# Three blocks of a fused retention and channel-mix kernel in 64-token chunks, and a new written order

## The chip, the cores and the metric

The kernel runs on one core of a Trainium2 chip. The metric is the time of one execution in microseconds on that core; runs of the kernel before gave 152.86 to 153.04 with a median of 152.95. PE is the matrix engine, DVE the vector engine, ACT the scalar engine; POOL (GpSimd) and SP issue the transfers here.

## The reference

Two layers follow each other. The first is a retention layer with 4 sequences, 8 heads, 768 tokens and a head size of 64: each head holds a 64x64 state that decays by a factor per token.

```python
state = gamma[None, :, None, None] * state + np.einsum('bhd,bhe->bhde', k[:, :, t], v[:, :, t])
y[:, :, t] = scale * np.einsum('bhd,bhde->bhe', q[:, :, t], state)
```

Its output, laid out as x of 4 x 768 x 512, goes through a channel mix:

```python
xk = mu_k * x + (1.0 - mu_k) * x_prev      # x_prev: x one token earlier
xr = mu_r * x + (1.0 - mu_r) * x_prev
k = np.maximum(xk @ w_k, 0.0)              # 512 -> 1024
v = k * k @ w_v                            # 1024 -> 512
r = 1.0 / (1.0 + np.exp(-(xr @ w_r)))
return r * v
```

Inputs and output are float32, and the products run on 16-bit operands.

## The kernel before

The 3072 tokens are worked in twelve blocks of 256; blocks 0 to 2 are the first sequence, 3 to 5 the second, and so on. `first(n)` is true for blocks 0, 3, 6 and 9, whose incoming state is zero; `more(n)` is false for 2, 5, 8 and 11, behind which no state is needed.

**The pieces.** A block goes through pieces with short names, each one function of the kernel. Loads `lq`, `lk`, `lv` bring q, k and v in. `vs` multiplies v by the decay of its place in the block. `Tq` and `Tk` turn q and k on PE into PSUM, and `Eq` and `Ek` copy the turned tiles back to 16 bits. `S` forms scores, `M` masks them into `a`. `C` forms the k-v products of each chunk, `U` adds them up to the state that is carried (`TG`, or `T32` for the last), and `G` decays it for the next block. `I`, `Y` and `J` form the output in PSUM: `I` and `J` from the carried state, `Y` from masked scores and values; where `Y` ends with the second half of the carried products, no `J` is written. `D` scales the output into `xT`. `dx` takes the difference of neighbouring tokens, `X.n.0.j` and `X.n.1.j` form the four pieces of xk and of xr. `K` multiplies by w_k, `Qa` and `Qb` apply relu and square on ACT, `R` and `s` form the gate, `V` multiplies by w_v, `O` multiplies by the gate, `st` stores. Blocks 3 and 4, 6 and 7, 9 and 10 share their mix products (`GROUPS`): `K.3`, `K.6` and `K.9` work on 512 tokens at once.

**Three ways to work a block.** Which one a block takes is set by tuples at the top. A block in neither `HALF` nor `WIDE` (0 and 1) has its tokens interleaved in pairs. A block in `WIDE` is cut into two chunks of 128 tokens, a block in `HALF` into four of 64.

- Scores: `WIDE` makes two pieces `S.n.0`, `S.n.1` of 8 products each, 64 rows by 128 columns on 128 tokens (L331), with one mask of 128x1024 for each (L354). `HALF` makes one piece of 32 products of 64x64 (L318), with one mask of 128x1024 (L347).
- State products: 8 or 16 with 128 rows (L384) against 24 or 32 with 64 rows (L366). `WIDE` adds up in two steps, `U.n.0` and `U.n.1`, `HALF` in four (three where no state follows), L419.
- Output: `WIDE` has `I`, `Y` with 16 products (L478) and `J`; `HALF` has `I` and a `Y` with 32 products (L462) that ends with what `J` does. The carried products stand on L441 in both. `D` is one operation of 128x1024 in `WIDE` (L514) and two of 128x512 in `HALF` (L507).
- Turning: a block in `WHOLE` has 16 products of 128 rows for each of q and k (L272), any other 32 of 64x64 (L278).

**The order.** No scheduler places the pieces. The kernel walks a string, `ORDER`, word by word, and each word issues one piece onto one engine's queue:

```python
for word in ORDER.split():
    word, _, at = word.partition("@")
    word, _, eng = word.partition("~")
    ...
    CODES[code](ENG.get(eng), *args)
```

`K.2.2@5` is a product into PSUM bank 5, `U.3.0~a` a sum on ACT; `~v` is DVE, `~p` POOL, `~s` SP. Each engine takes its own words in the order of the string and waits where an operand, a PSUM bank or a buffer isn't free. So the string decides what stands behind a waiting instruction. Buffers go round: four each of q, k and v, three of `vs`, of turned q and k and of `a`, four gates and four results.

Of the kernel before, what the change touches and what calls it, by code (L numbers as in the profile page):

```python
# [42 lines left out]
J.4 D.4~v dx.4~v R.2.0@6 Qb.2.1~a V.0.0.1 O.0.0~v X.3.0.1~v Eq.5~a Qb.1.2~a V.1.0.1 X.3.0.2~v
O.1.0~v Tq.6@01 Eq.6~a Tk.6@45 Ek.6~a st.0.0~s lk.7~p st.1.0~s V.1.1.0@3 V.1.1.1 O.1.1~v s.2.0~a
R.2.1@0 s.2.1~a lv.5~p X.3.0.0~v X.3.0.3~v Tk.7@67 Ek.7~a G.4~a S.6@45 M.6~v Tk.5@23 Ek.5~a vs.5~v
V.2.0.0@0 K.3.2@1 Qa.3.2~a K.3.0@6 S.5.0@23 M.5.0~v S.5.1@45 C.5@1 U.5.0~v K.3.3@7 Qb.3.2~a Qa.3.0~a
lq.7~p K.3.7@6 Qa.3.3~a Qa.3.7~a lv.6~p lq.8~p vs.6~v M.5.1~v V.2.0.1 st.0.1~s I.5@67 O.2.0~v
st.2.0~s C.6@23 U.6.0~a U.6.1~v U.6.2~v K.3.6@1 Qa.3.6~a lk.9~p X.3.1.3~v Y.5 Tq.7@45 Eq.7~a U.6.3~v
X.3.1.2~v I.6@01 J.5 X.3.1.0~v D.5~v X.3.1.1~v Qb.3.3~a G.6~a V.2.1.0@2 K.3.1@3 V.2.1.1 O.2.1~v
Qb.3.7~a Qa.3.1~a Qb.3.1~a dx.5~v K.3.4@4 K.3.5@5 Qa.3.5~a X.5.0.0~v X.5.0.3~v R.3.1@2 s.3.1~a  # L50
lv.7~p Qa.3.4~a X.5.0.1~v Qb.3.4~a R.3.0@5 R.4.0@2 s.3.0~a s.4.0~a Qb.3.0~a X.5.0.2~v vs.7~v K.5.2@4
S.7@67 st.1.1~s M.7~v Qb.3.5~a Y.6 Qb.3.6~a lv.10~p C.7@23 U.7.0~v X.5.1.1~v Qa.5.2~a K.5.0@5
R.4.1@6 Qa.5.0~a D.6~v s.4.1~a V.4.0.0@4 V.4.0.1 V.3.1.0@5 U.7.1~v Qb.5.0~a X.5.1.3~v U.7.2~v I.7@01
X.5.1.2~v U.7.3~v Tq.8@67 Eq.8~a X.5.1.0~v O.4.0~v lv.8~p vs.8~v Qb.5.2~a lq.10~p lk.8~p Tk.8@23
Ek.8~a V.3.1.1 V.3.0.0@4 C.8@67 O.3.1~v st.2.1~s st.3.1~s Y.7 dx.6~v D.7~v Tq.10@23 V.3.0.1 Eq.10~a
G.7~a dx.7~v X.6.0.2~v V.4.1.0@5 R.5.1@2 s.5.1~a K.5.3@0 Qa.5.3~a R.5.0@2 U.8.0~v O.3.0~v V.4.1.1
lv.9~p lk.10~p lq.9~p Tk.10@01 s.5.0~a U.8.1~v X.6.0.1~v Ek.10~a X.6.0.0~v Tk.9@23 Ek.9~a K.5.1@7
Qa.5.1~a X.6.0.3~v K.6.0@4 lq.11~p Qb.5.1~a Qa.6.0~a U.8.2~v I.8@01 vs.9~v S.8@23 M.8~v O.4.1~v
st.4.1~s K.6.4@7 Qa.6.4~a vs.10~v X.6.1.2~v K.6.2@6 C.9@23 Qa.6.2~a Qb.6.2~a U.9.0~a Y.8 U.9.1~v
D.8~v U.9.2~v U.9.3~v X.6.1.3~v Qb.5.3~a Tq.9@45 V.5.1.0@6 V.5.1.1 O.5.1~v Eq.9~a lk.11~p K.6.3@7  # L60
# [739 lines left out]
```

## Time and profile before

| | us |
|---|---|
| median of three runs | 152.95 |
| lowest, highest | 152.86, 153.04 |
| the profiled execution, its own time | 153.06 |
| span of that profile (first to last instruction) | 151.3 |
| PE busy | 143.5 |
| DVE busy | 127.5 |
| ACT busy | 103.4 |
| POOL busy | 55.3 |

The page gives times in microseconds, and mean durations of a group in nanoseconds. A line such as "L331 PE MATMUL ps<-qT,kT" names the kernel's line, the engine, the operation and what it writes from what. In a timeline the first number is the start, the second the time from the first start to the last end of so many like instructions, and a bracket holds idle time ahead of them and what ended it. The ends of products are modelled: a product's busy time is longer than the distance to the next one.

### The profile page before, as it was taken

How to read it: one execution, taken by the hardware profiler on the slowest of the kernel's cores; microseconds unless marked ns; L12 is line 12 of the kernel's file. 1: busy time of each engine (PE TensorE's matmuls, PEld its weight loads, DVE VectorE, ACT ScalarE, POOL GpSimd, SP SyncE). 2: the span in 40 equal slices, each digit the busy share in tenths (PEclk: the TensorE clock that was granted, in tenths of full speed). 3: DMA queues.
4: the chain of work that ended last, by engine and by line, in shares of the span. 5: the costliest groups of instructions: out<-in, count | busy, mean ns of one | idle time of the engine just before them, and what ended most of it. 6: DMA issues, size and time to landing. Idle time of an engine off the chain costs nothing.

```text
span 151.3 us, 5540 instructions
## 1 busy us (share of the span) xinstructions
PE 143.5 (95%) x2426; PEld 82.9 (55%) x2426; DVE 127.5 (84%) x212; ACT 103.4 (68%) x195; POOL 55.3 (37%) x65
## 2 busy tenths in 40 slices
PE   7878799999999999999999999999999999999991
PEld 3355487657754554547465564548456444655450
DVE  6976999999989999999999999999799999400432
ACT  3565979899844895879567786999504756839420
POOL 7954999479857209997700000000000000000000
PEclk9999999999999999999999999999999999999999
DMA  5999999999999999999999019311000005500433
GB/s 126 235 230 194 208 228 195 167 247 215 196 166 203 233 260 119 269 289 197 230 172 122 6 45 281 100 41 39 0 4 0 4 0 215 201 0 0 153 129 139
DMA packets 45624, 22.16 MB, mean 146 GB/s; under 512 B 37400, under 2 KB 41248, under 8 KB 45600
## 3 DMA queue, kind: packets, MB, share of 16 engines
q0 software_dynamic: 38704, 14.42, 74.5%
q1 hardware_dynamic: 6592, 7.21, 14.4%
q8 instruction: 19, 0.31, 0.8%
q10 hardware_dynamic: 304, 0.18, 0.6%
q14 instruction: 5, 0.04, 0.1%
HBM read 24.16 MB, written 6.29 MB: 201 GB/s over the span
## 4 chain that ended last, share of the span: by engine, by line
PE 86%; ACT 3%; DVE 3%; POOL 2%; DMA 2%; issue 1%; SPq 0%; DVEq 0%
PE ps L624 27%; PE ps L612 14%; PE ps L572 14%; PE ps L582 13%; PE ps L278 3%; PE ps L441 2%; DMA k2s<-in_k_dram 2%; PE ps L272 2%; DVE a L354 2%; PE ps L478 1%; ACT qT L241 1%; POOL vs L253 1%; PE ps L366 1%; PE ps L462 1%; PE ps L642 1%; POOL k L230 1%
## 5 line engine op out<-in xcount | busy, mean ns | idle before, releaser
L624 PE MATMUL ps<-wv,k2s 128*128 128x512 f16 x184 | 44.1, 380 | 0.0
L591 ACT ACTIVATE kr<-ps 128x512 f32<-128x512 f32 x48 | 27.8, 593 | 12.6 <-PE ps L582 6.6
L624 PEld LDWEIGHTS <-k2s 128*128 128x128 f16 x184 | 17.1, 98 | 18.9 <-ACT k2s L603 0.4
L630 DVE SCALAR_TENSOR_TENSOR os<-ps,rs 128x512 f32<-128x512 f32 x23 | 15.7, 684 | 11.9 <-ACT rs L618 9.4
L612 PE MATMUL ps<-wr,xr 128*128 128x512 f16 x96 | 23.5, 379 | 0.0
L582 PE MATMUL ps<-xk,wk 128*128 128x256 f16 x192 | 23.2, 273 | 0.0
L572 PE MATMUL ps<-xk,wk 128*128 128x512 f16 x96 | 23.0, 379 | 0.0
L618 ACT ACTIVATE rs<-ps 128x512 f32<-128x512 f32 x24 | 13.6, 597 | 12.9 <-PE ps L612 12.1
L230 POOL DMA_DIRECT2D k<-in_k_dram x20 | 17.7, 902 | 10.1 <-PE ps L384 6.8
L582 PEld LDWEIGHTS <-wk 128*128 128x128 f16 x192 | 18.1, 98 | 3.7
L241 ACT COPY qT<-ps 128x1024 f16<-128x1024 f16 (+1 forms) x13 | 12.3, 946 | 9.2 <-PE ps L278 7.8
L558 DVE SCALAR_TENSOR_TENSOR xr<-dx,mu,xT 128x256 f16<-128x256 f32 (+1 forms) x32 | 17.9, 577 | 0.1
L230 POOL DMA_DIRECT2D v<-in_v_dram x18 | 16.0, 911 | 3.9 <-DVE a L354 2.2
L558 DVE SCALAR_TENSOR_TENSOR xk<-dx,mu,xT 128x256 f16<-128x256 f32 (+1 forms) x32 | 17.0, 579 | 0.2
L354 DVE TENSOR_TENSOR a<-ps,c_sb 128x1024 f16<-128x1024 f32 (+1 forms) x14 | 14.6, 1066 | 0.7 <-PE ps L339 0.4
L603 ACT ACTIVATE k2s<-kr 128x512 f16<-128x512 f32 x24 | 14.8, 631 | 0.3
L612 PEld LDWEIGHTS <-xr 128*128 128x128 f16 x96 | 9.1, 98 | 10.7 <-issue 0.5
L572 PEld LDWEIGHTS <-wk 128*128 128x128 f16 x96 | 9.1, 98 | 10.5
L599 ACT ACTIVATE k2s<-kr 128x512 f16<-128x512 f32 x24 | 14.5, 627 | 0.3
L529 DVE TENSOR_TENSOR dx<-xT 128x1024 f32<-128x1024 f32 x11 | 13.4, 1222 | 0.2
L241 ACT COPY kT<-ps 128x1024 f16<-128x1024 f16 (+1 forms) x13 | 12.2, 944 | 1.9 <-PE ps L272 1.4
L253 DVE TENSOR_TENSOR vs<-v,csm_sb 128x1024 f16<-128x1024 f32 x10 | 12.2, 1217 | 0.0
(73 smaller groups left out, 165.3 us busy)
## 6 DMA issues: line engine op xcount, KB each, us to landing
out_dram<-os SPq DMA_DIRECT2D x23, 256.0 KB, 2.4
v<-in_v_dram POOLq DMA_DIRECT2D x18, 256.0 KB, 7.2
q<-in_q_dram POOLq DMA_DIRECT2D x11, 256.0 KB, 8.1
k<-in_k_dram POOLq DMA_DIRECT2D x21, 128.0 KB, 8.4
v<-in_v_dram POOLq DMA_DIRECT2D x2, 512.0 KB, 6.9
wk<-in_moe_w_k_dram POOLq DMA_DIRECT2D x2, 512.0 KB, 10.7
wv<-in_moe_w_v_dram POOLq DMA_DIRECT2D x2, 512.0 KB, 9.8
wr<-in_moe_w_r_dram POOLq DMA_DIRECT2D x1, 512.0 KB, 9.3
```

The costliest lines, as they stand in the source:

```text
L230: e.dma_start(out=dst[:, :, i * D : i * D + D], in_=src[:, i * P : i * P + P].rearrange("h p d -> p h d"),)
L241: e.copy(out=out, in_=in_)
L354: nc.vector.tensor_tensor(out=a_full(n)[:, i, :, j0:j1], in0=pairs(banks("S", n, i, j0))[:, :, j0:j1], in1=(below if wide(n) else causal[: ...
L558: nc.vector.scalar_tensor_tensor(out=XM[w](k)[:, j, t0:t1], in0=DX(k)[:, j, t0:t1], scalar=mu[:, w * NCO + j : w * NCO + j + 1], in1=x[:, ...
L572: nc.tensor.matmul(banks("K", n, g), lhsT=wk16[:, co, g * P : g * P + P], rhs=XM[0](k)[:, co, :], start=(co == 0), stop=(co == NCO - 1),)
L582: nc.tensor.matmul(pz[:, i, :], lhsT=wk16[:, co, fo * P : fo * P + P], rhs=XM[0](k)[:, co, m * TM + t0 : m * TM + t1], start=(i == 0 and c ...
L591: nc.scalar.activation(out=kr, in_=banks("K", n, g, *u), func=AF.Relu)
L599: nc.scalar.activation(out=k2s[:, n % 3 : n % 3 + 2, g, :], in_=kr, func=AF.Square,)
L603: nc.scalar.activation(out=K2(n)[:, w * g : w * g + w, t0:t1], in_=kr.rearrange("p a t -> p (a t)").rearrange("p (i t) -> p i t", i=w), fu ...
L612: nc.tensor.matmul(banks("R", n, tb), lhsT=XM[1](k)[:, co, t : t + P], rhs=wr16[:, co, :], start=(co == 0), stop=(co == NCO - 1),)
L624: nc.tensor.matmul(banks("V", n, tb), lhsT=K2(n)[:, fo, tb * P : tb * P + P], rhs=wv16[:, fo, :], start=(fo == 0), stop=(fo == NFO - 1),)
L630: nc.vector.scalar_tensor_tensor(out=OS(2 * n + tb), in0=banks("V", n, tb), scalar=1.0 / (KSC * KSC), in1=RS(2 * n + tb), op0=ALU.mult, op ...
```

## The change

The tuples put blocks 3, 4 and 5 with the blocks in four chunks. Block 2 is the only one left with two chunks, and block 3 is no longer turned with 128 rows:

```diff
-HALF = (6, 7, 8, 9, 10, 11)
+HALF = (3, 4, 5, 6, 7, 8, 9, 10, 11)
...
-WHOLE = (0, 1, 2, 3)
-WIDE = (2, 3, 4, 5)
+WHOLE = (0, 1, 2)
+WIDE = (2,)
```

No function changes. Loads have the same shapes, since k and v of a block in `WIDE` and of one in `HALF` are loaded alike. The string is the same up to the word `Qa.0.1~a`, and another one after it. Its first lines:

```diff
-K.0.2@1 Qa.0.0~a Qb.0.0~a Qa.0.2~a lq.3~p X.1.0.1~v X.1.0.3~v X.1.1.0~v Qa.0.1~a K.0.3@0 Qa.0.3~a
-lk.3~p vs.2~v Tq.2@1 X.1.1.2~v K.1.3@6 K.1.0@0 C.2@7 U.2.0~v lv.3~p Eq.2~a S.2.1@23 M.2.1~v S.2.0@45
...
-lq.5~p Ek.3~a K.2.2@5 Qa.2.2~a K.2.3@4 M.4.1~v M.4.0~v Qa.2.3~a Qb.2.3~a lk.6~p S.3.1@67 M.3.1~v
-S.3.0@01 vs.3~p C.3@23 U.3.0~a Qb.2.2~a K.2.1@4 Qa.2.1~a K.2.0@2 Qa.2.0~a I.3@45 lq.6~p vs.4~v
...
+K.0.2@1 Qa.0.0~a Qb.0.0~a Qa.0.2~a lq.3~p X.1.0.1~v X.1.0.3~v X.1.1.0~v Qa.0.1~a Tq.2@0 Eq.2~a
+Qb.0.2~a t.0.1.0~a K.0.3@2 K.1.1@3 Qa.1.1~a Qa.0.3~a Qb.0.3~a S.2.1@01 vs.2~v K.1.0@6 C.2@7 Tq.4@23
...
+J.2 Y.2 X.0.1.2~v R.0.1@6 Tq.3@45 lv.3~p D.2~v Qb.1.2~a Tk.4@23 dx.2~v X.2.0.3~v X.2.0.0~v X.2.0.2~v
+Ek.4~a Eq.3~a R.0.0@7 s.0.0~a lk.3~p X.2.0.1~v R.1.0@0 s.1.0~a Qb.1.0~a s.0.1~a S.4@23 K.2.0@7
+Tk.3@01 vs.3~v C.3@45 U.3.0~a M.4~v U.3.1~v U.3.2~v lv.4~p vs.4~v Ek.3~a Qa.2.0~a K.2.1@6 Qa.2.1~a
+wv.0~p U.3.3~v K.2.2@2 Qa.2.2~a S.3@01 M.3~v G.3~a K.2.3@7 Qa.2.3~a I.3@23 C.4@45 U.4.0~v V.0.1.0@6
...
```

Up to the first mix product on blocks 3 and 4 (`K.3.2` before, `K.3.0` after), both strings issue the mix products of blocks 0 to 2; the new one has the value groups up to `V.2.0.1` ahead of it where the old one has them up to `V.2.0.0`, and `S.6` and `Tk.6` behind it. On other engines, `vs.3` goes from POOL to DVE, and the decays `G.9` and `G.10` from ACT to DVE; `G.3` and `G.4` stay on ACT. On POOL, v of block 3 is now asked for ahead of its k, and the later loads come in another order. The end:

```diff
-O.9.0~v R.11.1@4 V.10.1.1 Qb.11.1~a V.11.0.0@7 R.11.0@5 s.11.0~a st.9.0~s Vc.11.1.1@1 s.11.1~a
-O.10.1~v st.10.1~s Oc.11.1.1~v V.11.0.1 O.11.0~v st.11.0~s sc.11.1.1~a Vc.11.1.0@4 Oc.11.1.0~v
+s.11.1~a Vc.11.1.1@4 V.11.0.0@7 O.10.1~v Oc.11.1.1~v O.10.0~v st.10.0~s st.10.1~s V.11.0.1 s.11.0~a
+O.11.0~v st.11.0~s Vc.11.1.0@6 sc.11.1.1~a Oc.11.1.0~v sc.11.1.0~s
```

Built, the new program has 2647 products in place of 2423 on PE (a group of products with a 32-bit operand counted as written): 224 more, all of them of the small kind. It has three masks fewer, six state sums more, and `vs.3`, `G.9` and `G.10` more on DVE.

More of the change, by code (lines that the diff above doesn't have):

```diff
@@ L43 @@
[L43 to L60, printed above, removed]
@@ new lines @@
+Tk.6@45 Ek.6~a K.3.1@0 Qa.3.1~a Qb.3.1~a X.3.1.3~v K.3.4@1 Qa.3.4~a M.5~v st.0.1~s K.3.7@0 lv.6~p
+Qb.3.6~a X.3.1.1~v vs.6~v X.3.1.0~v K.3.2@6 Qa.3.7~a Y.5 S.6@01 Qb.3.4~a Qb.3.3~a C.6@45 vs.7~v
+Qa.3.2~a Qb.3.2~a M.6~v U.6.0~a U.6.1~v V.2.1.0@7 V.2.1.1 O.2.1~v lk.9~p lq.7~p Qb.3.7~a U.6.2~v
+lk.8~p D.5~v K.3.5@6 R.4.0@0 s.4.0~a Qa.3.5~a U.6.3~v V.4.0.0@4 Tq.7@01 dx.5~v X.5.0.2~v X.5.0.1~v
+Eq.7~a st.1.1~s G.6~a X.5.0.0~v C.7@23 U.7.0~v X.5.0.3~v I.6@67 R.3.0@5 s.3.0~a U.7.1~v R.4.1@0
+s.4.1~a U.7.2~v lq.8~p lq.10~p R.3.1@1 K.5.2@5 s.3.1~a U.7.3~v S.7@01 M.7~v Qa.5.2~a Qb.5.2~a Y.6
@@ new lines @@
+I.7@23 Qb.3.5~a K.5.1@5 Qa.5.1~a V.4.0.1 K.5.3@5 Qa.5.3~a Qb.5.3~a D.6~v X.5.1.1~v st.2.0~s O.4.0~v
+Qb.5.1~a Tk.8@67 Ek.8~a lv.8~p vs.8~v Y.7 D.7~v V.3.1.0@5 dx.6~v K.5.0@4 Qa.5.0~a dx.7~v X.6.0.1~v
+X.6.0.0~v Tq.8@01 lq.11~p X.6.0.2~v Eq.8~a lq.9~p Tq.9@67 Eq.9~a X.5.1.2~v X.6.0.3~v Tk.9@23
+Qb.5.0~a V.3.0.0@4 V.3.0.1 V.4.1.0@6 V.4.1.1 C.8@01 Ek.9~a G.7~a O.3.0~v U.8.0~v Tq.10@23 Eq.10~a
+U.8.1~v V.3.1.1 O.3.1~v U.8.2~v K.6.1@7 Qa.6.1~a st.2.1~s Qb.6.1~a O.4.1~v K.6.4@4 Qa.6.4~a
+V.5.1.0@7 X.6.1.3~v I.8@01 lv.9~p S.8@23 lk.11~p Tk.11@45 Ek.11~a K.6.0@6 Qa.6.0~a Qb.6.0~a lk.10~p
@@ new lines @@
+V.5.1.1 X.6.1.2~v M.8~v Tk.10@45 Ek.10~a Tq.11@23 Y.8 Eq.11~a lv.10~p K.6.5@6 st.3.1~s X.6.1.0~v
+Qa.6.5~a X.6.1.1~v Qb.6.5~a K.6.6@4 X.5.1.3~v vs.9~v K.6.3@5 X.5.1.0~v R.5.1@6 s.5.1~a Qa.6.3~a
+Qb.6.3~a R.5.0@2 s.5.0~a vs.10~v D.8~v K.6.2@6 Qa.6.2~a O.5.1~v dx.8~v R.6.0@5 s.6.0~a X.8.0.2~v
+C.9@23 U.9.0~a S.10@01 S.9@67 X.8.0.0~v U.9.1~v M.9~v V.5.0.0@5 V.5.0.1 Qa.6.6~a Qb.6.6~a K.6.7@4
+Qa.6.7~a X.8.1.1~v U.9.2~v U.9.3~v R.6.1@2 X.8.0.1~v X.8.0.3~v K.8.0@4 M.10~v Qa.8.0~a s.6.1~a
+Qb.6.7~a st.3.0~s O.5.0~v K.8.1@3 C.10@01 G.9~v U.10.0~v U.10.1~v U.10.2~v Qa.8.1~a Qb.6.2~a I.9@45
@@ new lines @@
+S.11@67 M.11~v K.8.2@2 R.7.0@3 Qa.8.2~a Qb.8.0~a K.8.3@2 V.6.0.0@0 s.7.0~a Qa.8.3~a I.10@23 lv.11~s
+U.10.3~v vs.11~v G.10~v Y.9 D.9~v Qb.8.3~a Qb.6.4~a C.11@67 V.6.1.0@1 V.6.1.1 V.7.0.0@4 U.11.0~v
+U.11.1~v U.11.2~v I.11@67 Y.10 V.6.0.1 Qb.8.1~a V.8.1.0@5 dx.9~v X.8.1.0~v D.10~v st.5.1~s dx.10~v
+X.9.0.1~v st.4.0~s Qb.8.2~a V.8.1.1 O.6.0~v X.9.0.3~v V.7.1.0@2 V.7.0.1 X.9.1.2~v X.9.0.0~v
+X.9.0.2~v V.7.1.1 R.7.1@0 s.7.1~a O.7.1~v V.8.0.0@3 st.5.0~s Y.11 K.9.1@0 Qa.9.1~a K.9.2@2 Qa.9.2~a
+Qb.9.2~a K.9.3@0 D.11~v K.9.5@2 X.8.1.2~v V.8.0.1 X.8.1.3~v X.9.1.1~v K.9.7@6 X.9.1.0~v dx.11~v
@@ new lines @@
+X.11.0.2~v X.11.0.3~v O.7.0~v Qa.9.3~a X.11.1.2~v X.11.1.0~v R.8.0@0 Qa.9.5~a X.9.1.3~v X.11.0.1~v
+Qb.9.3~a s.8.0~a K.9.0@2 K.9.4@0 Qb.9.1~a Qa.9.4~a K.9.6@4 Qa.9.0~a Qa.9.6~a Qb.9.6~a R.8.1@0
+Qa.9.7~a Qb.9.7~a X.11.1.3~v X.11.1.1~v R.11.0@2 X.11.0.0~v K.11.0@4 K.11.1@6 Qb.9.4~a Qa.11.1~a
+st.7.0~s st.4.1~s O.6.1~v st.6.1~s Qb.11.1~a Qa.11.0~a R.10.0@1 Qb.9.0~a R.9.0@6 st.7.1~s K.11.2@7
+st.6.0~s Qb.9.5~a V.9.1.0@4 V.9.1.1 s.8.1~a O.8.1~v V.9.0.0@5 V.9.0.1 R.9.1@0 O.8.0~v s.9.1~a
+s.9.0~a st.8.0~s s.10.0~a Qa.11.2~a Qb.11.2~a V.10.1.0@3 V.10.1.1 O.9.0~v O.9.1~v st.9.1~s st.9.0~s
@@ L81 @@
+V.10.0.0@6 R.10.1@7 K.11.3@4 s.10.1~a Qb.11.0~a st.8.1~s Qa.11.3~a Qb.11.3~a V.10.0.1 R.11.1@7
+s.11.1~a Vc.11.1.1@4 V.11.0.0@7 O.10.1~v Oc.11.1.1~v O.10.0~v st.10.0~s st.10.1~s V.11.0.1 s.11.0~a
+O.11.0~v st.11.0~s Vc.11.1.0@6 sc.11.1.1~a Oc.11.1.0~v sc.11.1.0~s
 """
```

32 lines of the change are left out of this document (8 added, 24 removed).

## The prediction

> **What bounds the kernel now.** I read the page's busy table first, then the table of ten-microsecond stretches, and then the timelines of PE and DVE.
>
> ```profile
> PE 143.5 (95%) x2426; PEld 82.9 (55%) x2426; DVE 127.5 (84%) x212; ACT 103.4 (68%) x195; POOL 55.3 (37%) x65
> ```
>
> ```profile
> 20.00:30.00 10.00, 10.00 (x161) 7.95 (x159) 9.85 (x16) 8.84 (x18) 7.13 (x9) 1.00 1.67 197
> 30.00:40.00 10.00, 9.74 (x168) 6.74 (x167) 9.93 (x14) 9.68 (x17) 8.81 (x10) 1.00 1.30 223
> ...
> 120.00:130.00 10.00, 10.00 (x49) 4.56 (x48) 9.82 (x19) 6.88 (x14) 0.00 (x0) 1.00 0.31 117
> 130.00:140.00 10.00, 10.00 (x64) 6.01 (x62) 0.59 (x2) 7.04 (x15) 0.00 (x0) 1.00 0.11 41
> ```
>
> The columns are length, then busy time of PE, PEld, DVE, ACT and POOL, the granted clock (1.00 throughout), DMA share and GB/s. In these stretches PE is busy in all but 0.26 us. DVE is at 9.8 to 9.9 of 10 up to 130 us, and then falls to 0.59. So two engines run side by side at their limit: PE sets the end, because 18 us of products are left when DVE is done, and DVE feeds PE with almost nothing to spare until then. ACT is full only from 30 to 40 us (9.68). A change here is worth what it takes from PE, as long as DVE can deliver sooner by as much.
>
> **Prices on PE.** A busy time holds the drain of the last product, so I take the distance from one group's start to the next one's.
>
> ```profile
> 28.23 0.31 PE L441 MATMUL ps<-qT,tg 64*64 64x128 f16 x8
> 28.36 0.42 PE L278 MATMUL ps<-c_sb,q 64*64 64x64 f16 x32
> 28.74 0.64 PE L478 MATMUL ps<-a,vs 128*64 128x128 f16 x16
> 29.31 1.04 PE L612 MATMUL ps<-wr,xr 128*128 128x512 f16 x4
> ...
> 30.55 0.28 PE L441 MATMUL ps<-qT,tg 64*64 64x128 f16 x8
> 30.77 2.76 PE L612 MATMUL ps<-wr,xr 128*128 128x512 f16 x12
> 33.46 0.62 PE L331 MATMUL ps<-qT,kT 64*128 64x128 f16 x16
> 34.01 0.64 PE L272 MATMUL ps<-c_sb,q 128*64 128x128 f16 x16
> 34.48 0.61 PE L272 MATMUL ps<-c_sb,k 128*64 128x128 f16 x16
> 35.03 1.92 PE L582 MATMUL ps<-xk,wk 128*128 128x256 f16 x16
> ...
> 37.76 0.44 PE L384 MATMUL ps<-vs,k 128*64 128x64 f16 x16 [0.26 <-POOL vs L253]
> 38.14 1.92 PE L582 MATMUL ps<-xk,wk 128*128 128x256 f16 x16
> ...
> 48.80 0.44 PE L278 MATMUL ps<-c_sb,q 64*64 64x64 f16 x32
> 49.08 0.44 PE L278 MATMUL ps<-c_sb,k 64*64 64x64 f16 x32
> 49.44 0.82 PE L624 MATMUL ps<-wv,k2s 128*128 128x512 f16 x3
> ...
> 86.93 0.33 PE L441 MATMUL ps<-qT,tg 64*64 64x64 f16 x16
> 87.08 0.44 PE L318 MATMUL ps<-qT,kT 64*64 64x64 f16 x32
> 87.45 1.90 PE L572 MATMUL ps<-xk,wk 128*128 128x512 f16 x8
> 89.28 0.45 PE L366 MATMUL ps<-vs,k 64*64 64x64 f16 x32
> 89.56 0.46 PE L462 MATMUL ps<-a,vs 64*64 64x64 f16 x32
> 89.84 0.32 PE L441 MATMUL ps<-qT,tg 64*64 64x64 f16 x14
> ```
>
> A small group that stands last before large products takes some 0.1 more (48.80 to 49.08 is 0.28, the same form before L624 0.36). I take that 0.1 off each group and count it apart.
>
> - **Scores**, blocks 3 to 5: two 128-wide halves in 16 products take 0.55 (33.46 to 34.01), 32 quarter products 0.37 - 0.1 = 0.27 (87.08 to 87.45). Three blocks: -0.28 x 3 = -0.84.
> - **Transposes** of block 3, which leaves WHOLE: 0.47 + 0.55 - 0.1 = 0.92 becomes 0.28 + 0.36 - 0.1 = 0.54: -0.38.
> - **State** products: 0.38 - 0.1 (37.76 to 38.14) against 0.28 (89.28 to 89.56) is nothing in blocks 3 and 4; block 5 needs no last state, a little less, -0.05.
> - **Mix of carried state and values** (I, Y, J): wide 0.13 + (0.57 - 0.1) + (0.22 - 0.1) = 0.72. Half: 0.15 (86.93 to 87.08) for I, 0.28 for the values (89.56 to 89.84) and, for the products inside Y that were J's, no more than I's 0.15: 0.58. -0.14 each for blocks 4 and 5. Block 3 begins a sequence and multiplies with no incoming state; it has 12 + 12 quarter products there instead of 16 + 16: -0.2. Together -0.48.
> - **Runs.** The new order has 26 small-after-large turns against 25: +0.1 before and +0.1 after, say +0.15.
>
> Sum: -0.84 - 0.38 - 0.05 - 0.48 + 0.15 = **-1.6 us** of PE time. Large products are the same in number. The bounds: with no allowance for the 0.1 the scores and mix are worth about 0.2 more, -1.8; a group whose successors are all large saves 0.1 less each time, -1.2.
>
> [...] The rows give 32 products of 64x64 in 0.27 to 0.28 us, 8 to 9 ns apart. [...]
>
> **DVE.** The same blocks change DVE's list.
>
> ```profile
> L354 DVE TENSOR_TENSOR a<-ps,c_sb 128x1024 f16<-128x1024 f32 x10 | 12.0, 1219 | 0.3 <-PE ps L331 0.2
> L253 DVE TENSOR_TENSOR vs<-v,csm_sb 128x1024 f16<-128x1024 f32 x10 | 12.2, 1217 | 0.0
> L419 DVE TENSOR_TENSOR tg<-ps,tg 128x256 f16<-128x256 f32 x20 | 8.4, 418 | 0.5 <-ACT tg L424 0.2
> ...
> L507 DVE TENSOR_TENSOR xT<-ps,gy_sb 128x512 f32<-128x512 f32 x12 | 8.3, 690 | 0.7
> ...
> L630 DVE SCALAR_TENSOR_TENSOR os<-ps,rs 128x512 f32<-128x512 f32 x23 | 15.7, 684 | 11.9 <-ACT rs L618 9.4 <-PE ps L624 2.3
> ```
>
> Over the kernel: three masks fewer (-3.66), six state sums more (+2.51), three outputs in two pieces of L507 instead of one of 1.22 (43.90 below; 3 x 0.16 = +0.48), vs.3 comes from POOL (+1.22), and the decays G.9 and G.10 come from ACT; a DVE decay is not in the trace: between nothing and the 0.69 of twice its elements in L507, I take the row of the same 128x256, the state sum, 2 x 0.42 = +0.84. Sum **+1.4 us**, on an engine with nothing free. ACT loses its eight short decays of blocks 9 and 10 near 100 us, where the DVE and PE queues set the pace: worth nothing.
>
> Where this bites is found by comparing the two queues at one place: the first product with block 3's and 4's mixed input, which PE cannot start before DVE's third xk piece and cannot finish without the fourth.
>
> ```profile
> 43.90 1.23 DVE L514 TENSOR_TENSOR xT<-ps,gy_sb 128x1024 f32<-128x1024 f32 x1 [0.23 <-PE ps L478]
> ...
> 52.41 1.40 DVE L558 SCALAR_TENSOR_TENSOR xk<-dx,mu,xT 128x512 f16<-128x512 f32 x2
> ```
>
> ```profile
> 53.95 1.89 PE L572 MATMUL ps<-xk,wk 128*128 128x512 f16 x8
> ```
>
> *PE's side.* It got there at 53.95. In the new order it has done one value group more by then (+0.87), S.6 and Tk.6 less (-0.37, -0.36), C.5 more (+0.2), it has no POOL wait (-0.26), and it has saved scores (-0.56), transposes (-0.38) and mixes (-0.14 - 0.2) of blocks 3 and 4. It arrives at 53.95 - 1.2 = 52.75.
>
> *DVE's side.* The fourth xk piece ended at 53.81. In the new order DVE has by then done two more vs (3 and 5, +2.43), two masks fewer (-2.44), four sums more (+1.67), two split outputs (+0.32) and one result fewer (-0.68): +1.3. Its waits for PE up to there, 0.23 at 43.90 and small ones, fall away as PE comes earlier: I allow 0.5 to 0.8. It ends at 54.3 to 54.6. The product on that piece is the last of four, 0.65 after the group's start, so the group can start at 53.65 to 53.95 where PE stands ready at 52.75: PE loses **0.9 us** (0.5 to 1.4) between about 34 and 54 us. ACT, full at 9.68 in 30 to 40 us, still must turn block 3 and 4's four transposes and decay both there, and holds PE by a like amount at the same place; two shortages at one place do not add.
>
> Further on the same comparison gives smaller shortages (block 5's first products 0.6 to 0.8), which the earlier 0.9 covers.
>
> **Sum:** -1.6 + 0.9 = -0.7, and the POOL wait of 0.26 at 37.76 goes with vs.3's move, partly inside what DVE then gates: -0.15. Together -0.85. The end is unchanged in form: the last two value halves, a result and a store, and this tail stays. The profiled execution took 153.06, 0.11 above the median of the runs (152.95), with a span of 151.3: it would become 152.2 with a span of 150.45, and the median **152.1 us**.
>
> What POOL no longer does (1.92 us for vs.3, below) I count at nothing: POOL waited 3.8 us for that load and has only loads to issue. SP's queue, stores and block 11's v, is moved too. The order asks for that v a block ahead of its use, so it is hidden behind blocks 8 to 10; were it not, vs.11 and all of DVE's list behind it would wait by as much.
>
> **Rivals.**
>
> *PE alone counts.* DVE's shortage is absorbed, because pieces that are ready are placed in between. For it: PE's queue was full beside a DVE at 9.8. Against it: the 0.9 above is a sum of work, not of waits. Time: 152.95 - 1.8 = 151.15; I give 0.17.
>
> *DVE sets the end.* From the start of the changed part to the last mixed piece, DVE has the +1.4 and two results fewer (-1.37) before it, so it ends as late as now if its present waits recur. Below, the last mixed pieces end at 129.61. In the new order the last is block 11's first xk piece, and behind its product PE has 21 groups of 0.87, 18.2 us: 129.65 + 18.2 = 147.85; in the row shown last, the present one ends at 147.05 + 0.87 = 147.92. Then nothing is gained: 152.9. For it: DVE's 9.82 in 120 to 130. Against: its waits for PE should shrink. 0.17.
>
> ```profile
> 128.74 0.87 DVE L558 SCALAR_TENSOR_TENSOR xr<-dx,mu,xT 128x256 f16<-128x256 f32 x2
> ```
>
> ```profile
> 147.05 1.04 PE L642 MATMUL ps<-wv,k2s 128*128 128x256 f16 x8
> ```
>
> *A load comes late: slower.* Block 3's k is now asked for behind its v.
>
> ```profile
> 35.79 1.92 POOL L253 TENSOR_TENSOR vs<-v,csm_sb 128x1024 f16<-128x1024 f32 x1
> ```
>
> ```profile
> POOL vs L253 <- DMA v<-in_v_dram: 3.8, 1, 3.8
> ```
>
> That vs waited 3.8 us for v, so the last of the four transfers lands at 35.8. In the new order this last one is k, and PE comes to its transposes at about 35.5 to 36. Each microsecond more is paid in full, since everything on PE stands behind Tk.3. It turns the forecast into a loss from 1.15 us late on, landing after 37.0; at 2 us late the time is 154.1. 0.13.
>
> *Quarter products do not overlap as well* with other neighbours. By busy time the 64x64 ones below cost 21 ns each, the 64x128 ones 42: 432 x 21 = 9.1 us against at most 212 x 42 = 8.9. [...]
>
> ```profile
> L441 PE MATMUL ps<-qT,tg 64*64 64x64 f16 x176 | 3.7, 197 | 0.0
> ...
> L441 PE MATMUL ps<-qT,tg 64*64 64x128 f16 x80 | 3.4, 222 | 0.5 <-DVE tg L419 0.5
> ```
>
> **Numbers.** The forecast, 151.6 to 152.6, has 0.48; 0.02 is left for the rest. About 0.2% (0.3 us) is what a measurement here tells from no change. Faster: 0.48 + 0.17 + 0.07 of the DVE case = 0.72; same 0.10; slower 0.08 under 153.4 and 0.10 above it, 0.18. The range runs from PE alone to the late load at 1.3 us: 151.1 to 153.4.
>
> **What would show it.** Right: L318 and L347 with three groups more, L331 at 16 products, small groups at the distances above; PE idle of 0.5 to 1.4 us between 25 and 55 us, released by DVE or ACT, and DVE idle under 0.3 there; the first product on blocks 3 and 4 at 53.6 to 54. Wrong: a PE or DVE wait for a DMA after 30 us; PE idle after 60 us above 0.5; DVE's last mixed piece at or after 129.6; quarter groups at over 0.4 us.

## The result, and the profile after

The changed kernel takes **159.5 us** (median of 4 runs, 159.34 to 161.31) beside 153.0 for the kernel before in the same session: a ratio of 1.0455, 95% interval [1.0361, 1.0549]. The forecast was 152.1, in a range of 151.1 to 153.4. The ratio is that of the means, without one run of the kernel before, which took 156.08 where the other three took 152.86 to 153.04. The change is 4.6% slower, and the text below tells why. The profiled execution took 159.39 with a span of 157.6, 6.3 more than the span before.

First the page of the kernel after: its busy line and the share of engines in the chain that ended last.

```profile
PE 143.1 (91%) x2650; PEld 82.3 (52%) x2650; DVE 128.4 (81%) x221; ACT 102.1 (65%) x187; POOL 53.5 (34%) x64
...
PE 73%; DVE 16%; issue 6%; ACT 3%; DVEq 0%
```

PE still makes up most of the chain. DVE has 0.9 us more work (1.4 was forecast) on a span 6.3 longer; its share of the chain went from 3% to 16%. What is new is "issue", 6% of the chain, time in which an engine waited for nothing that the profile shows. The table of stretches of the kernel after (length, then busy time of PE, PEld, DVE, ACT and POOL, granted clock, DMA share, GB/s) says when.

```profile
20.00:30.00 10.00, 10.00 (x152) 7.51 (x150) 9.93 (x17) 9.20 (x19) 7.26 (x9) 1.00 1.59 211
30.00:40.00 10.00, 8.52 (x245) 5.60 (x245) 8.64 (x13) 8.24 (x15) 7.05 (x9) 1.00 1.40 215
40.00:50.00 10.00, 7.33 (x180) 4.07 (x165) 7.74 (x15) 5.78 (x16) 6.82 (x8) 1.00 1.76 210
50.00:60.00 10.00, 9.73 (x220) 5.21 (x220) 9.17 (x15) 5.40 (x7) 2.49 (x4) 1.00 0.71 117
60.00:70.00 10.00, 8.62 (x223) 4.58 (x222) 8.64 (x13) 8.39 (x15) 5.68 (x7) 1.00 1.53 200
70.00:80.00 10.00, 9.13 (x210) 5.50 (x209) 8.52 (x16) 6.78 (x14) 6.84 (x8) 1.00 1.31 212
80.00:90.00 10.00, 10.00 (x276) 6.11 (x274) 9.72 (x15) 8.46 (x15) 2.00 (x3) 1.00 1.08 118
```

PE has lost 6.7 us, all of it between 30 and 80 us, which is while the loads run, mostly at some 200 GB/s. From 80 to 90 us it has more products than in any earlier stretch (276) and loses nothing: many small products alone did no harm here. Nor did they where loads run, if they stood in the right places, as a stretch of the kernel before shows:

```profile
70.00:80.00 10.00, 10.00 (x329) 6.11 (x329) 9.69 (x17) 7.03 (x12) 4.65 (x6) 1.00 1.87 205
```

In the stretches where PE loses time DVE and ACT are idle too (7.74 and 5.78 of 10 from 40 to 50 us), so neither of them holds PE up. The waits of PE, by line (total, times, longest):

```profile
PE ps L365 <- issue: 2.9, 2, 2.1
PE ps L277 <- issue: 2.0, 2, 1.1
PE ps L317 <- issue: 1.4, 1, 1.4
```

Together 6.3 us, in five waits on three lines: state, transposes, scores. PE's timeline of the kernel after, at these places and at two that serve as a measure:

```profile
35.97 0.22 PE L277 MATMUL ps<-c_sb,k 64*64 64x64 f16 x4
37.33 0.41 PE L277 MATMUL ps<-c_sb,k 64*64 64x64 f16 x28 [1.14 <-issue]
37.56 0.45 PE L365 MATMUL ps<-vs,k 64*64 64x64 f16 x32
...
41.14 0.32 PE L440 MATMUL ps<-qT,tg 64*64 64x64 f16 x12
43.53 0.45 PE L365 MATMUL ps<-vs,k 64*64 64x64 f16 x32 [2.07 <-issue]
...
46.15 0.31 PE L440 MATMUL ps<-qT,tg 64*64 64x64 f16 x12
46.39 1.04 PE L611 MATMUL ps<-wr,xr 128*128 128x512 f16 x4
...
49.08 0.32 PE L277 MATMUL ps<-c_sb,q 64*64 64x64 f16 x16
50.27 0.32 PE L277 MATMUL ps<-c_sb,q 64*64 64x64 f16 x16 [0.87 <-issue]
50.40 0.44 PE L461 MATMUL ps<-a,vs 64*64 64x64 f16 x32
...
58.27 2.80 PE L571 MATMUL ps<-xk,wk 128*128 128x512 f16 x12
...
61.00 0.44 PE L317 MATMUL ps<-qT,kT 64*64 64x64 f16 x32
61.27 0.32 PE L440 MATMUL ps<-qT,tg 64*64 64x64 f16 x16
...
65.76 0.32 PE L317 MATMUL ps<-qT,kT 64*64 64x64 f16 x16
67.46 0.32 PE L317 MATMUL ps<-qT,kT 64*64 64x64 f16 x16 [1.38 <-issue]
67.59 0.44 PE L365 MATMUL ps<-vs,k 64*64 64x64 f16 x32
...
72.66 0.40 PE L365 MATMUL ps<-vs,k 64*64 64x64 f16 x28
73.93 0.22 PE L365 MATMUL ps<-vs,k 64*64 64x64 f16 x4 [0.87 <-issue]
73.96 0.32 PE L440 MATMUL ps<-qT,tg 64*64 64x64 f16 x12
...
153.32 1.04 PE L641 MATMUL ps<-wv,k2s 128*128 128x256 f16 x8
```

Four of the five waits stand in the middle of a group: PE does 4 of 32 transposes, or 28 of 32 state products, stops for a microsecond, and goes on. The products of a group read the same tiles and write the same banks, so missing data is an unlikely cause. Two inputs that could have been late were there: the second half of block 3's k, of which the group at 35.97 had still to read, landed at 34.7, and the `vs` of block 4, which the state products at 43.53 read, was done at 40.5. The brackets hold less than the loss, as a product's drain counts as busy (the 32 products at 61.00 are busy for 0.44 us, and the next group starts after 0.27). By distances, against 0.27 for 32 quarter products (61.00 to 61.27) and 0.24 for twelve before large ones (46.15 to 46.39): 1.59 - 0.27, 2.39 - 0.24, 1.32 - 0.27, 1.83 - 0.27 and 1.30 - 0.27, in sum **7.1 us**. From the first product on block 0's mixed input (19.47 before, 19.39 after) to the last group (147.05 and 153.32) the new kernel takes 6.35 more. So without these five waits it would have been 0.76 ahead, or less, as the waits also gave DVE and ACT time to catch up.

**Theory F** (F for fetch): PE stands still because its own next instructions have not yet come. The profile's page lists the DMA queues. Before and after, the line of the instructions' queue is

```profile
q8 instruction: 19, 0.31, 0.8%
```

```profile
q8 instruction: 20, 0.33, 0.8%
```

(packets, MB, share). That is 16 KB a packet, and before some 128 products to a packet (2426 over 19, of which the busy line has as many weight loads). I numbered PE's instructions in the built program (a product and its weight load are two) and set the packets' times from the trace beside the moment at which PE passed each 256th number. All five waits begin at the same remainder, 184 (numbers 1208, 1464, 1720, 2488, 2744). Counted in the rows of the trace 606, 734, 862, 1246 and 1374 products stand ahead of them, each 94 above a multiple of 128. From these numbers I take a packet to be a page of 256 instructions, 64 bytes each (16 KB over 256), or 128 products with their weight loads (from here on "page" alone means this). By the rows below PE runs on one page while the packet of the next comes: that of 40.38 to 41.36 came while PE worked on the page from 37.23 to 45.73. Some of these pages, in us:

```
           page begun  next packet from, to   next page begun   page lasted
before        37.23        40.38   41.36          45.73             8.5
              45.73        48.30   49.36          52.25             6.5
              70.82        75.29   76.39          78.15             7.3
after         30.38        34.70   36.01          37.33 stall       7.0
              37.33        41.17   42.11          43.53 stall       6.2
              43.53        48.01   48.98          50.27 stall       6.7
              61.27        65.03   65.98          67.46 stall       6.2
              67.46        71.45   72.35          73.93 stall       6.5
              99.95        99.43  100.69         107.50             7.6
```

While loads run, a packet in these rows starts 2.6 to 4.5 us after PE began the page before it, takes 0.9 to 1.3 us, and in these rows PE goes on no sooner than 1.3 us behind its end. The five pages ahead of the waits held 4.1 to 5.9 us of work (what they lasted less the wait); they were used up first, and PE waited. Where the loads pause, it did not: the packet behind the page begun at 56.58 started 1.06 us after it, in a slice in which the profile has 7 GB/s, and that page of 4.7 us passed without a wait; so did the one begun at 73.93, of 4.8 us, whose packet started 2.2 us after it. Behind the loads a packet started even before the page ahead of it was begun (last row: 99.43 and 99.95). Before, the pages between 30 and 75 us hold 6.0 to 8.5 us of work, so the fetches stay hidden, but by little: the closest page (78.15) was begun 1.8 us behind its packet's end, 0.5 more than the 1.3 at a wait. After, 124 more products stand ahead of the first product on blocks 3 and 4 (1074 in place of 950), and the pages of the same stretch hold, less the waits, only 4.1 to 6.3 us of work. The profile names no cause for these five waits, and nothing in the kernel's text shows where a page ends.

### The profile page after: what moved, and what is told of

Its sections match the earlier page's. It is cut to its first block, busy times and chain, and to the rows that moved or that the text cites. A ratio compares the mean times of both kernels' runs of the same rounds, so it can differ in the third digit from the quotient of the medians.

```text
span 157.6 us, 5982 instructions
## 1 busy us (share of the span) xinstructions
PE 143.1 (91%) x2650; PEld 82.3 (52%) x2650; DVE 128.4 (81%) x221; ACT 102.1 (65%) x187; POOL 53.5 (34%) x64
## 4 chain that ended last, share of the span: by engine, by line
PE 73%; DVE 16%; issue 6%; ACT 3%; DVEq 0%
PE ps L623 20%; PE ps L611 13%; PE ps L581 12%; PE ps L571 12%; PE ps L277 4%; DVE xT L506 3%; PE ps L440 2%; PE ps L365 2%; DVE a L353 2%; DVE gy_sb L727 2%; DVE dx L528 2%; PE ps L317 1%; DVE vs L252 1%; DVE tg L418 1%; DVE xk L557 1%
## 5 line engine op out<-in xcount | busy, mean ns | idle before, releaser
L623 PE MATMUL ps<-wv,k2s 128*128 128x512 f16 x184 | 43.6, 380 | 0.0
L581 PE MATMUL ps<-xk,wk 128*128 128x256 f16 x192 | 23.9, 273 | 0.4 <-ACT rs L617 0.3
L557 DVE SCALAR_TENSOR_TENSOR xr<-dx,mu,xT 128x256 f16<-128x256 f32 (+1 forms) x32 | 17.3, 577 | 0.0
L506 DVE TENSOR_TENSOR xT<-ps,gy_sb 128x512 f32<-128x512 f32 x18 | 12.4, 687 | 2.1 <-PE ps L440 1.2
L418 DVE TENSOR_TENSOR tg<-ps,tg 128x256 f16<-128x256 f32 x26 | 10.9, 419 | 3.7 <-PE ps L365 2.1
L234 POOL DMA_DIRECT2D q<-in_q_dram x12 | 10.7, 904 | 8.2 <-PE ps L365 7.5
```

What stands on the lines that cost most here:

```text
L506: nc.vector.tensor_tensor(out=x[:, :, :, v], in0=banks("I", n)[:, v].rearrange("p (j i t) -> p j i t", j=NJ, i=2), in1=g[:, :, :, v], op=A ...
L557: nc.vector.scalar_tensor_tensor(out=XM[w](k)[:, j, t0:t1], in0=DX(k)[:, j, t0:t1], scalar=mu[:, w * NCO + j : w * NCO + j + 1], in1=x[:, ...
L581: nc.tensor.matmul(pz[:, i, :], lhsT=wk16[:, co, fo * P : fo * P + P], rhs=XM[0](k)[:, co, m * TM + t0 : m * TM + t1], start=(i == 0 and c ...
L623: nc.tensor.matmul(banks("V", n, tb), lhsT=K2(n)[:, fo, tb * P : tb * P + P], rhs=wv16[:, fo, :], start=(fo == 0), stop=(fo == NFO - 1),)
```

## The experiments

Times are medians; each experiment ran beside the kernel before on the same chip (153.1 to 153.4 in all sessions).

**1. Move the page boundaries, leave the work.** At the very start 64 small products (`y`, weights of 128x128 on 4 columns) stand in place of two of the 32-bit zero products (four of the trace's: x2 in place of x6 on L702); all that follows stands 120 instructions, or 60 products (the expectation has 56), later.

```diff
-z.12@6
+z.4@6 y.64@6
```

> The changed kernel with 64 tiny products (128x128 weights, 4 columns) at the start in place of eight of the start's 128-column products, so that every later product stands 56 products later in PE's program, and the order of the work is the same. Theory F (PE waits for the next 256 of its own instructions): in the changed kernel all five gaps stood where the count of PE's instructions, weight loads and products together, is 184 above a multiple of 256. Here the same count has to give the gaps, so they move by about 56 products: the gaps inside Tk.3 (L277, 1.14 us at 37.3), C.4 (L365, 2.07 at 43.5), Tq.5 (L277, 0.87 at 50.3), S.6 (L317, 1.38 at 67.5) and C.7 (L365, 0.87 at 73.9) are gone and others of 0.5 to 2.5 us with the releaser issue stand in other groups, at 184 above a multiple of 256. Sum of these gaps 4 to 9 us, time 158 to 162 us. Rival (those five groups wait for data, for a copy or a load): the gaps stay in those five groups, time 159.5 plus or minus 0.3.

Measured: 167.0 us, above the 158 to 162 expected. PE's timeline of this kernel:

```profile
34.98 0.37 PE L277 MATMUL ps<-c_sb,k 64*64 64x64 f16 x24
35.84 0.26 PE L277 MATMUL ps<-c_sb,k 64*64 64x64 f16 x8 [0.50 <-issue]
...
41.77 1.03 PE L581 MATMUL ps<-xk,wk 128*128 128x256 f16 x8 [0.49 <-DVE tg L418]
...
51.74 0.22 PE L277 MATMUL ps<-c_sb,q 64*64 64x64 f16 x3
53.88 0.56 PE L277 MATMUL ps<-c_sb,q 64*64 64x64 f16 x28 [1.93 <-issue]
54.37 3.37 PE L623 MATMUL ps<-wv,k2s 128*128 128x512 f16 x8
```

All five old waits are gone: block 3's transposes, split at 4 of 32 before, run through here, and block 4's are split at 24 of 32. Seven others have come, 8.4 us by their brackets. One of them carries the name of a DVE tile (41.77), yet its instruction stands at the common remainder too: at such a place the named releaser is not to be trusted. The number at which they begin is the same as without the edit: in the rows of the trace the six up to 90 us have 606, 734, 862, 990, 1502 and 1630 products ahead of them, all 94 above a multiple of 128, as the five waits of the changed kernel do (remainder 184 in the numbering above). The rival, that those groups waited for data, is out.

Of the 8.4 us between the two profiled executions (167.8 and 159.39) the start has 3.0 (first product on mixed input at 22.42 in place of 19.39), the waits 2.1, and the clock the rest. The slow start is a cost of the edit itself: the early products ran slower (two zero products of 128x512 take 1.01 us at 13.27, and 0.61 at 9.27 in the changed kernel), after 64 narrow products in the place of two long ones. Three stretches of the table of this kernel:

```profile
52.00:54.00 2.00, 0.12 (x13) 0.11 (x16) 1.79 (x4) 0.15 (x1) 0.00 (x0) 0.99 1.30 218
54.00:56.00 2.00, 2.00 (x32) 0.89 (x28) 0.32 (x1) 1.52 (x2) 0.00 (x0) 0.50 0.51 174
56.00:58.00 2.00, 2.00 (x7) 0.78 (x6) 0.22 (x1) 0.41 (x1) 0.00 (x0) 0.65 0.03 8
```

Behind a wait of 1.93 us the granted clock is 0.50, and eight large products take 3.37 us in place of 1.9 (54.37, above). The other long wait, of 2.00 at 87.50, is followed by 0.53 and 0.62 in the next two such stretches. The mean clock of this run, 0.979, is worth 0.021 x 166.0 = 3.5 us.

**2. Take loads away.** The loads of q, k and v of blocks 6 to 11 are dropped, after and before; these blocks compute on what the buffers hold. The words taken from the order, here of the kernel after:

```diff
-lq.6~p
...
-lk.7~p lv.7~p
...
-lv.11~s
```

> The changed kernel without the loads of q, k and v of blocks 6 to 11: these blocks compute on what the buffers hold, so their outputs are not the reference's. Loads then end near 47 us. Theory F says that the instructions are fetched slowly only while loads fill the DMA engines: the gaps near 37 and 43 us stay (3.2 us together), those near 50, 67 and 74 us (3.1 us) shrink to under 0.5 together; time 156 to 157 us. Rival (PE's sequencer itself is slow at these places, whatever the DMA does): all five gaps stay, time 159 to 159.6. Second rival (only the load of the data is late): gaps of the blocks whose load is kept stay as well, but then the releaser would be a DMA and not issue.

> The kernel before without the loads of q, k and v of blocks 6 to 11, which compute on what the buffers hold. Theory F: the kernel before had no wait for instructions after 20 us, so the loads cost PE nothing: 152.4 to 153.1 us. Rival (the loads slow engines in some other way, by access to the memory on the chip): faster by over 0.7 us, and the gain of the changed kernel without the same loads is then partly that.

Measured, after: 157.8, four runs of 155.22 to 160.24, the two slower ones with a mean clock of 0.978. In the profiled one (155.22, clock 1.0) only one wait is left:

```profile
40.57 0.32 PE L440 MATMUL ps<-qT,tg 64*64 64x64 f16 x12
42.69 0.45 PE L365 MATMUL ps<-vs,k 64*64 64x64 f16 x32 [1.79 <-issue]
```

Those at 50, 67 and 74 us are gone, as expected; the DMA traffic, 218 GB/s from 30 to 40 us, was 117 from 40 to 50 us and 29 from 50 to 60. The one at 37 us left no bracket either, which I had not expected; its group took 0.47 (36.52 to 36.99) in place of 0.27. Before: 153.4, the same within its interval [0.9985, 1.0041]: the loads cost the kernel before, with pages of 6.0 us and more between 30 and 75 us, nothing. So PE's sequencer is not slow by itself at these numbers: without loads beside them three waits (0.87, 1.38 and 0.87) are gone. That fits packets that the loads delay. From the first mix product to the last group the two kernels differ by 1.8 us (129.1 against 127.3), and this one wait is 1.9 of it by distances (2.12 - 0.24): without it, and the 0.2 at 36.52, the change gains 0.1 to 0.3 us here.

**3. Add products to the kernel before.** The transposes of blocks 3 to 6 are issued twice, 224 products.

```diff
-            for j in range(j0, j1):
+            for j in [x for x in range(j0, j1) for _ in range(2 if n in (3, 4, 5, 6) else 1)]:
```

> The kernel before with each transpose of blocks 3 to 6 issued twice in a row (the same result is written twice): 224 small products more, the number by which the changed kernel has more, with no other change. By the distances of the timeline the second issue costs 0.37 to 0.47 us a group in place of the time of nothing: 1.9 to 2.9 us, 154.9 to 155.9. Theory F: groups of small products then follow each other closely while loads run, and waits of 0.3 to 2 us with the releaser issue come in between 30 and 75 us: 3 to 5 us on top, 157 to 161. Rival (the changed kernel's loss comes from its order or its tiles): no gap with the releaser issue over 0.2 us, 154.9 to 155.9.

Measured: 165.1 us, ratio 1.0675 [1.0627, 1.0723], more than expected; the two runs with a full clock took 163.5 and 164.0. PE's timeline in the first of four new waits:

```profile
34.23 0.51 PE L331 MATMUL ps<-qT,kT 64*128 64x128 f16 x12
36.34 0.29 PE L331 MATMUL ps<-qT,kT 64*128 64x128 f16 x4 [1.60 <-issue]
```

It stands within a score group of 128-wide tiles which this edit doesn't touch, again at remainder 184 (606 products ahead in the rows of the trace). The four waits (1.6, 2.4, 1.1, 3.3) come to 8.3 us where I had expected 3 to 5. Neither the new tiles nor the new order is needed for the loss: more products in the load's time suffice.

**4. The fetch alone.** A probe with all loads and, on PE, nothing but 3200 products of 64x64 on zeros; no other part of the computation is done.

> A probe with the loads of the kernel before, all issued in a row, and beside them nothing on PE but 50 groups of 64 products of 64x64 on zeros (3200 products, 6400 instructions with their weight loads); no other part of the computation is done, zeros are stored. By the rows of the kernel before, 32 such products take 0.27 to 0.28 us, so 128 products (256 instructions) take 1.1 us. Theory F: after each 256 instructions PE waits for the next ones, with a period of 5.5 to 6.5 us (a gap of 4.4 to 5.4) as long as the loads run, and with a shorter one of 2.5 to 4 us behind them; the 25 pages take 110 to 150 us. Rival (products alone cost PE time, fetches are hidden): no regular gaps, 27 to 30 us for all products.

Its timeline where the loads end (212 GB/s from 60 to 75 us, 5 from 90 to 110):

```profile
65.42 1.92 PE L666 MATMUL ps<-zero 64*64 64x64 f16 x128 [4.82 <-issue]
72.16 1.92 PE L666 MATMUL ps<-zero 64*64 64x64 f16 x128 [4.83 <-issue]
78.63 1.92 PE L666 MATMUL ps<-zero 64*64 64x64 f16 x128 [4.55 <-issue]
82.36 1.92 PE L666 MATMUL ps<-zero 64*64 64x64 f16 x128 [1.81 <-issue]
85.81 1.92 PE L666 MATMUL ps<-zero 64*64 64x64 f16 x128 [1.53 <-issue]
```

Here the page shows itself: 128 products, a wait, 128 products. The period is 5.9 to 7.3 us beside the loads (5.5 to 6.5 was expected) and 3.5 to 4.0 without, and the granted clock was 0.50 in both stretches. The 25 pages end at 127 us, within the 110 to 150 expected; the rival, 27 to 30 us, is far off.

**5. Fewer products in the changed kernel.** Blocks 3 to 8 are turned with 128 rows, 192 products less.

```diff
-WHOLE = (0, 1, 2)
+WHOLE = (0, 1, 2, 3, 4, 5, 6, 7, 8)
```

> The changed kernel with the transposes of blocks 3 to 8 done with 128 rows (16 products a group in place of 32): 192 products fewer on PE in the same order of work, and twelve groups that each cost more array time, 0.55 in place of 0.36 us (distances of the timeline of before, 34.01 to 34.48 against 48.80 to 49.08): +2.2 us of array time. Theory F: pages of 256 instructions then hold more large products and last longer, so the waits with releaser issue (7 us in the changed kernel) fall to 1 to 4 us: 155.5 to 159. Rival (small products cost only their array time): 161.0 to 162.

Measured: 162.2 us (161.05 to 163.53), which is the rival's number, and theory F's was missed. The waits at page ends fell only from 6.3 to 5.1 us (1.06, 2.14, 0.82, 1.12 in the profiled run), and the array time of 2.2 us, as priced, came on top. The theory stands, since all four waits are at remainder 184, but my use of it failed: what counts is each page by itself and not the mean, and even with 192 products fewer some pages are still too short. The profile names DVE tiles for two of the four (2.14 and 1.06); all four begin 94 above a multiple of 128 in the rows of the trace (862, 1118, 1502 and 1758 ahead), so here too the name is not to be trusted.

**6. The tiles alone.** Old order, each piece at its old place, new tiles for blocks 3 to 5; and for block 5 alone.

```diff
-HALF = (6, 7, 8, 9, 10, 11)
+HALF = (3, 4, 5, 6, 7, 8, 9, 10, 11)
...
-S.3.1@67 M.3.1~v S.3.0@01
+S.3@67 M.3~v
```

> The kernel before in its own order of work, with only the tiles of blocks 3 to 5 changed (four 64-token chunks, 64x64 scores, block 3 turned in 64 rows), each piece at its old place, on banks that are free there. It has the changed kernel's number of products. By the prediction's prices PE saves 1.75 us, and DVE has three masks less and six sums more. Theory F: the number of PE instructions between 25 and 75 us sets the waits, whatever the order: gaps with releaser issue of 2 to 7 us in sum, time 154 to 159. Rival (the new order is at fault, the tiles gain): no such gap above 0.2 us, 151.2 to 152.5.

> The same with the tiles of block 5 alone changed, in the order of before. PE saves 0.4 us by the prediction's prices (0.28 scores, 0.14 mix). Theory F: block 5's small products fall at about 55 to 62 us, where the kernel before has pages that last 6.1 to 6.5 us, and 60 products more shorten these; waits of 0 to 1.5 us, time 152.5 to 154.3. Rival (tiles gain, order is at fault): 152.4 to 152.7, without any gap with releaser issue above 0.2 us.

Measured: 164.9 us for three blocks (161.1 to 167.6; mean clocks of 0.999 down to 0.979), 161.4 for block 5 alone (156.67 to 163.97; clocks of 1.0 to 0.965). Two waits of the first and one of the second, in their profiled runs (161.1 and 156.67):

```profile
53.12 0.26 PE L275 MATMUL ps<-c_sb,k 64*64 64x64 f16 x8 [1.67 <-issue]
...
85.93 0.32 PE L459 MATMUL ps<-a,vs 64*64 64x64 f16 x16 [1.92 <-issue]
```

```profile
82.39 0.45 PE L275 MATMUL ps<-c_sb,q 64*64 64x64 f16 x32 [1.65 <-issue]
```

At remainder 184 the first has five waits of 5.0 us in sum up to 86 us (606, 862, 990, 1502 and 1630 products ahead in the trace's rows), the second three of 2.6 (990, 1374 and 1502). So the tiles cost the time without the new order; the new order, at 159.5, is the better one for these tiles. The new order with the old tiles was not run. In the first, waits of PE for DVE and ACT add 3.0 us, so its loss is not one of pages alone. That 64 products more in one block already cost 3.4 us in the best run (156.67 against a median of 153.24 before) shows how little in hand the kernel before has. Both went beyond what I expected, already in the runs at a full clock: 161.1 against 154 to 159, and 156.67 against 152.5 to 154.3. The clock adds to it: at 0.965 of the full clock 163.97 us hold 0.035 x 162 = 5.7 us of lost clock, of the 7.3 by which that run is longer.

**7. What in the loads delays the packets.** The probe again with other loads: weights alone on GpSimd's queue, 512 KB each; v alone on SyncE's. Again nothing else is computed.

> The probe of 3200 products of 64x64 again, nothing else of the computation done, with other loads beside it: only the three weights, over and over, 40 loads of 512 KB on the queue of GpSimd, whose rows in memory are the longest of the kernel's loads. The first probe had gaps of 4.0 to 5.4 us while all kinds of loads ran and 1.5 to 2.1 behind them. If the bytes in flight set the wait for instructions, the gaps under these loads are 4 us and more again; if the many packets under 512 bytes of q, k and v set it, they are under 3 us.

> The same probe with only the loads of v, 36 blocks' worth (the twelve blocks three times) on SyncE's queue. Their rows are short, like those of k and v in the kernel. If the queue of GpSimd is what delays the instructions, the gaps are 1.5 to 2.5 us as behind the loads; if short packets or any full DMA queue delay them, 4 us and more while these loads run.

One wait of each, from the middle of its loads (all others beside loads were 4.00 to 4.69 in the first, 2.08 to 3.75 in the second):

```profile
66.93 1.93 PE L666 MATMUL ps<-zero 64*64 64x64 f16 x128 [4.00 <-issue]
```

```profile
66.94 1.92 PE L666 MATMUL ps<-zero 64*64 64x64 f16 x128 [2.90 <-issue]
```

Both move some 200 GB/s beside these waits (207 from 60 to 75 us in the first, a mean of 194 over the second). Neither of the second probe's two forecasts came (1.5 to 2.5 us, or 4 and more). Short packets are not needed for the long waits, since the weights have few of them (1168 of 24744 packets under 512 bytes; 63024 of 72265 in the second probe), and the rate does not set the difference. With the loads on SyncE's queue PE waits less than with them on GpSimd's, where the first probe, with all kinds of loads, had 4.00 to 5.37. This is one run of each, and the kinds of loads differ as well as the queues, so that it is the queue is likely but not shown.

**8. Use it.** v of blocks 6 to 10 is asked for on SyncE's queue, after and before.

```diff
-lv.6~p lv.7~p lv.8~p lv.9~p lv.10~p
+lv.6~s lv.7~s lv.8~s lv.9~s lv.10~s
```

> The changed kernel with the loads of v of blocks 6 to 10 asked for on SyncE's queue and not on GpSimd's, at the same places of the order; nothing else changes. In the probes the gaps beside loads on SyncE's queue were 2.1 to 3.7 us, beside loads on GpSimd's 4.0 to 5.4. Theory F: from 47 us on less of the traffic stands in GpSimd's queue, the packets of instructions come sooner, and the gaps behind 55 us (1.4 at S.6, 0.9 at C.7) shrink to under 0.8 together, those at 37 and 43 us (3.2) stay: 157 to 159 us. Rival (queue is of no account in a kernel whose DMA is full either way): 159 to 160 us.

> The same edit in the kernel before, as a control: it had no wait for instructions there, so nothing is to be gained. Theory F: 152.8 to 153.5 us. Rival (v on SyncE's queue comes late behind a store that waits, or early enough to help DVE): off by more than 0.5 us either way, and then the number for the changed kernel has that in it too.

Measured: 170.2 and 159.6 us, both worse: the control's rival, v that comes late behind a store. One row of each kernel's timeline:

```profile
76.19 0.64 PE L365 MATMUL ps<-vs,k 64*64 64x64 f16 x32 [8.55 <-DVE vs L252]
```

```profile
74.68 0.45 PE L366 MATMUL ps<-vs,k 64*64 64x64 f16 x32 [2.92 <-DVE vs L253]
```

SyncE is held by stores that wait for results (100.4 us in eight waits for DVE's result, after), and v behind them comes late: after, v of block 6, for whose `vs` the first of these rows waits, is asked for at 62.1 us in place of 48.5. The wait at 50 us is gone and the one in S.6 shrank from 1.38 to 0.75, but two new ones at page ends came at 88.27 and 95.02 (0.66 and 1.07). This doesn't show that SyncE's queue delays packets less: around 50 us v of blocks 6 and 7 had not been asked for (they were at 62.1 and 54.3), so there was less to load. As a remedy it would need loads that no store stands before; that wasn't tried. No version beat the kernel before.

## Why the prediction was wrong

- **PE's sum, -1.6 us: the step that failed.** It priced 224 more products by the array time of their groups, and took the instructions themselves to cost nothing. The rows for it were all from places where the fetch kept up. The runs put a term of +7.1 us beside it, and say what it hangs on: pages of 256 instructions (experiments 1 and 4) fetched beside loads (2 and 4), filled with small products (3 and 6). A smaller slip in the sum: its -0.2 for block 3's carried products compares with a block that has an incoming state, but the kernel before, too, does only half of them there (4 where block 4 has 8), so about -0.1 was due.
- **The rest of the sum, -0.85.** The price of a small group held: 32 quarter products in scores took 0.27 (61.00 to 61.27). Taking the five waits out, the kernel after is 0.76 us ahead; experiment 2, with less to take out, gives 0.1 to 0.3. So without waits a gain of 0.1 to 0.8 stands beside the forecast 0.85, below it.
- **DVE's shortage of 0.9 us at the first product on blocks 3 and 4.** That product started at 58.27. Less the first three waits by distances (1.32 + 2.15 + 1.05 = 4.5) it is 53.75, within the 53.65 to 53.95 forecast. That fits, but the waits gave DVE time to catch up, so it is no proof that DVE gated it; it wasn't tested by itself.
- **The POOL wait, -0.15**, is gone as forecast: after 20 us no PE row of the kernel after has POOL as releaser.
- **The late load of block 3's k**, the main rival on the slower side: it didn't happen. That k had landed at 34.7, and block 3's transposes began at 35.97 and stopped there for 1.14 us at the end of a page: the forecast place, another cause.
- **Quarter products that don't overlap**: out, by the 0.27 above. **DVE sets the end**: out, though DVE was close: PE idled 0.14 us in all from 110 to 150 us, and the end is PE's, as before.
- The signs: of those named for "right", the idle time of PE released by DVE or ACT came to one wait of 0.34 (for ACT, 34.92). Of those named for "wrong", PE idle after 60 us above 0.5 came in at 2.25 us (1.38 and 0.87). DVE's last mixed piece ended at 135.0, later than the 129.6 named, but by less than the waits ahead of it, and one wait of DVE for a DMA came, 3.5 us for a store at 150.82, while PE was at work. What the profile of before did show, and I passed over, is the queue of instructions with its 19 packets, for the 2426 products of the busy line: 128 to a packet. It showed no wait, and so its margin of 0.5 us went unasked.

## What to carry to other kernels

Small products had a price here beside their engine's time, that of their own instructions. With the loads of q, k, v and weights beside it, PE got 256 instructions (128 products with weight loads) every 5.9 to 7.3 us in the first probe, and in the kernel after five pages with 4.1 to 5.9 us of work ran out; so in a kernel like this one a stretch under load should have no page with less work than that. Before splitting tiles, add up the work of each page of 128 products; the count in a stretch does not tell, since the kernel before has 329 in ten microseconds under load and loses nothing. Split where loads have ended: behind 74 us the kernel after has no wait of this kind. A wait inside a group of like products, with "issue" as its releaser, at multiples of one distance in the count (128 products here), is the sign of it, and a few idle products at the program's start that move the place of the waits are the cheapest test, if the large products there are left as they are (in experiment 1 the start cost 3.0 us).
